# First batch's chain rebuilt in a sketched-attention and FFN kernel: float32 Gram rest, shared key grid, ScalarE rounding the queries, two-step denominator

## The chip, the cores and the metric

The kernel runs on one core of one Trainium2 chip. The time is that of one execution on the device in microseconds (us); a kernel's time is the median of its executions. TensorE is PE below, with PEld its weight loads; VectorE is DVE, ScalarE is ACT, GpSimd is POOL.

## The reference

Attention with a sketched polynomial feature map, then a multiplicative FFN on its output (four batches, four heads, 1088 tokens, head size 32, sketch rank r = 8):

```python
def phi(x):                       # 64 features per token
    a = np.einsum('rd,bhsd->bhsr', S1, x)
    b = np.einsum('rd,bhsd->bhsr', S2, x)
    return np.einsum('bhsi,bhsj->bhsij', a, b).reshape(*x.shape[:-1], r * r)
q_p, k_p = phi(q), phi(k)
kv  = np.einsum('bhsf,bhsd->bhfd', k_p, v)
z   = np.sum(k_p, axis=2)
num = np.einsum('bhsf,bhfd->bhsd', q_p, kv)
den = np.einsum('bhsf,bhf->bhs', q_p, z)[..., None] + 1e-06
x   = (num / den)                 # heads side by side: 4352 x 128
out = ((x @ w1) * (x @ w2)) @ w3 @ w_out
```

S1, S2 and the FFN weights arrive as 64-bit floats.

## The kernel before

The denominator can be near zero, so the kernel computes it in float32 pairs. It needs z, which it gets from the Gram matrix of k (32 x 32 per head) through two small chains, T = S x Gram and N = P x T; P comes from S alone. The Gram itself is exact because k is split into a leading part on a coarse grid and a rest. This is where the change works. "The Gram" below also includes the `kv` products, which sum in the same PSUM tile `ps_kvz`.

```python
def lead(kf, tiles, name, eng):                        # split of k
    x = {n: tiles.tile(kf.shape, t, ...) for n, t in (("k1", BF16), ("k2", F32), ("ks", F32))}
    # peak: row maximum; first: k1 = k rounded to the grid; second:
    nc.vector.tensor_sub(x["k2"], kf, x["k1"])
    eng.tensor_add(x["ks"], kf, x["k1"])
...
def gram(chunks, rows, first, last):
    def products(out, lhs, rhs, start):
        for i, c in enumerate(chunks):
            for h in range(H):                         # the heads rotate innermost
                nc.tensor.matmul(out[h*D:(h+1)*D], c[lhs][rows, h], c[rhs][rows, h], ...)
    products(acc["kv"], "v", "kp", first)              # 64 columns, float32
    products(acc["g2"], "k2", "ks", False)             # 32 columns, float32
    products(acc["g1"], "k1", "k1", False)             # 32 columns, bf16
...
def lead_q():                                          # split of a q tile, on VectorE
    round_to(s["q1"], s["qT"], grid(s["qT"], 128, 8, "q"))
    (nc.vector if lean else nc.gpsimd).tensor_sub(s["q2"], s["qT"], s["q1"])
```

A 64-bit weight becomes float32 in three steps: `words` (two ScalarE activations), `join` (VectorE) and `add` (VectorE). With `signs` a third ScalarE step casts the sign, and the join is one operation; without it VectorE does a shift-and-mask as well.

An FFN step computes `a_ps` and `b_ps` (each one float32 matmul of 512 columns, run as two instructions); ScalarE copies a, VectorE multiplies by b. The third product `ps_o` follows with a lag of 16 steps, since the weights w3 x w_out (`w3o`) have to be built first. The first part of the program has a fixed order; later parts merge several streams of steps in proportion:

```python
run_all([sketch_pairs, ..., kv0, q_tr, kv1, kvr, ..., f[0], n_ay1, ..., n_phT, f[5], n_nd])
run(merge([(1.7, x) for x in f[6:]] + ffn_steps(1, 16), k_steps(1), w_out))
```

## Time and profile before

320.8 us, the median of the runs (319.51 to 322.37). The trace is of a run of 322.2 us, with a span of 320.4 us. The four stages below are read from starts of named matmuls, on the time axis of the views; only PE's end is an end. "Step 7" ends, here and below, with the start of its last instruction, 0.6 us before that is done. The prediction shows the lines themselves.

| stage of the kernel before | from, us | to, us | length |
|---|---|---|---|
| serial chain to the first FFN product | 0 | 41.0 | 41.0 |
| first eight FFN steps (0 to 7) | 41.0 | 62.3 | 21.3 |
| building w3 x w_out ("conversion stage") | 62.3 | 117.3 | 55.0 |
| FFN, with k and q of the later batches between | 117.3 | 315.1 | 197.8 |

In the last stage TensorE is nearly always busy, so every instruction added to it there costs its own time. Until 41.0 us it is busy for 31.0 us, of which some 12 are padding; in the second stage for 18.9 of 21.9 us.

### The profile page before, as it was taken

The page shows a single profiled execution, that of the slowest core. Times are in us where ns is not written, and L with a number is a line of the kernel's source. Part 1 is how long each engine was busy: PE and PEld are TensorE (multiplying, and loading weights), DVE is VectorE, ACT ScalarE, POOL GpSimd, SP SyncE. Part 2 cuts the span into 40 slices and gives each one's busy share as a digit, 9 for nine tenths or more (in the row PEclk, how much of TensorE's full clock was granted, in tenths as well). Part 3 has the DMA queues.
Part 4 walks back from the last instruction along what each step waited for, and adds up shares of the span by engine and source line. Part 5 has one row for each costly group of instructions (what it writes and reads, how often), then busy time and mean ns, then how long its engine had stood idle before and what let it go on. Part 6 is the DMA issues. An engine that isn't in the chain of part 4 may idle for free.

```text
span 320.4 us, 4951 instructions
## 1 busy us (share of the span) xinstructions
PE 293.6 (92%) x1924; PEld 174.4 (54%) x1924; DVE 195.3 (61%) x495; ACT 132.7 (41%) x258; POOL 16.6 (5%) x21
## 2 busy tenths in 40 slices
PE   7866997669998999999999999999999999999992
PEld 5746553257766765465645446555454644444581
DVE  6987867996879638376846626654572572462130
ACT  4313273897998330533332253322324224323231
POOL 2200000100003000010301001000100100000000
PEclk9855699978999999999999999999999999999998
DMA  5998240375743000000000000000000000000000
GB/s 165 337 264 243 94 133 0 105 266 163 246 156 118 0 0 2 33 1 2 3 33 2 0 33 0 2 2 35 2 0 0 33 0 2 33 0 1 35 33 17
DMA packets 15064, 20.77 MB, mean 65 GB/s; under 512 B 4032, under 2 KB 11456, under 8 KB 15040
## 3 DMA queue, kind: packets, MB, share of 16 engines
q1 hardware_dynamic: 15040, 20.46, 19.9%
q8 instruction: 15, 0.25, 0.3%
q14 instruction: 9, 0.07, 0.1%
HBM read 18.22 MB, written 2.23 MB: 64 GB/s over the span
## 4 chain that ended last, share of the span: by engine, by line
PE 73%; ACT 11%; DVE 10%; issue 4%; POOL 1%; DVEq 0%; POOLq 0%
PE ps_o L740 19%; PE a_ps L727 15%; PE b_ps L731 14%; PE ps_w3o L375 3%; PE ps_x L682 3%; ACT cv_c L230 3%; PE ps_kvz L474 3%; PE ps_c L610 3%; PE ps_ph L665 2%; PE ps_c L608 2%; PE idle_ps L184 2%; ACT sgn L236 2%; PE ps_ab L424 2%; ACT cv_m L231 1%; ACT ffa L729 1%
## 5 line engine op out<-in xcount | busy, mean ns | idle before, releaser
L733 DVE TENSOR_TENSOR ab<-ffa,b_ps 128x512 f32<-128x512 f32 (+1 forms) x72 | 47.2, 655 | 62.5 <-PE b_ps L731 56.9
L729 ACT COPY ffa<-a_ps 128x512 f32<-128x512 f32 (+1 forms) x72 | 40.7, 565 | 78.3 <-PE a_ps L727 73.4
L727 PE MATMUL a_ps<-xT,w 128*128 128x512 f32 (+1 forms) x144 | 72.4, 585 | 0.7 <-ACT xT L685 0.7
L731 PE MATMUL b_ps<-xT,w 128*128 128x512 f32 (+1 forms) x144 | 70.5, 571 | 1.3 <-ACT ffa L729 1.3
L740 PE MATMUL ps_o<-ab,w3o 128*128 128x512 f32 (+1 forms) x144 | 70.3, 582 | 0.7 <-ACT ob L743 0.7
L731 PEld LDWEIGHTS b_ps<-xT,w 128*128 128x128 f32 x144 | 26.7, 190 | 29.4 <-issue 22.7
L740 PEld LDWEIGHTS ps_o<-ab,w3o 128*128 128x128 f32 x144 | 24.8, 190 | 22.6 <-issue 20.2
L727 PEld LDWEIGHTS a_ps<-xT,w 128*128 128x128 f32 x144 | 24.4, 192 | 18.0 <-issue 11.7
L375 PE MATMUL ps_w3o<-wo,w3T 128*128 128x128 f32 x128 | 18.0, 293 | 2.4 <-ACT w3T L370 1.7
L264 DVE TENSOR_REDUCE g_q<-qT 128x1 f32<-128x512 f32 (+1 forms) x9 | 5.9, 655 | 23.3 <-ACT qT L578 23.3
L375 PEld LDWEIGHTS ps_w3o<-wo,w3T 128*128 128x128 f32 x128 | 16.9, 205 | 5.5 <-ACT w3T L370 2.8
L667 ACT COPY pT<-ps_ph 128x512 f32<-128x512 f32 (+1 forms) x18 | 9.2, 565 | 15.8 <-PE ps_ph L665 15.8
L231 ACT ACTIVATE cv_m<-raw 128x512 int32<-128x512 uint32 x22 | 15.4, 698 | 0.8 <-DVE w3c L248 0.8
L230 ACT ACTIVATE cv_c<-raw 128x512 f32<-128x512 f32 x22 | 15.4, 706 | 0.0
L610 PE MATMUL ps_c<-Rl,qT 128*128 128x96 f32 (+1 forms) x72 | 15.0, 302 | 0.0
L608 PE MATMUL ps_c<-Rf,q 128*128 128x64 f32 (+1 forms) x72 | 13.2, 276 | 1.4 <-POOL q L584 1.4
L584 POOL TENSOR_TENSOR q<-qT,q 128x512 f32<-128x512 f32 (+1 forms) x6 | 6.4, 1073 | 150.1 <-DVE q L275 150.1
L608 PEld LDWEIGHTS ps_c<-Rf,q 128*128 128x128 f32 (+1 forms) x72 | 11.4, 201 | 4.3 <-issue 2.4
L236 ACT CAST sgn<-cv_c 128x512 f16<-128x512 f32 x17 | 13.4, 790 | 0.1
L184 PE MATMUL idle_ps<-zeros 128*128 128x256 bf16 x52 | 11.9, 420 | 1.6 <-DVE zeros L179 1.6
L665 PEld LDWEIGHTS ps_ph<-ident,ph 128*128 128x128 f32 x68 | 7.9, 143 | 7.6 <-issue 5.9
L432 DVE TENSOR_TENSOR kp<-ps_ab,b_sb 128x1024 f32<-128x1024 f32 x8 | 9.8, 1222 | 3.5 <-ACT b_sb L428 3.5
(169 smaller groups left out, 372.8 us busy)
## 6 DMA issues: line engine op xcount, KB each, us to landing
raw<-in_moe_w_dram SPq DMA_DIRECT2D x20, 512.0 KB, 4.5
k_sb<-in_k_dram SPq DMA_DIRECT2D x4, 512.0 KB, 5.1
v_sb<-in_v_dram SPq DMA_DIRECT2D x4, 512.0 KB, 5.8
q_sb<-in_q_dram SPq DMA_DIRECT2D x4, 512.0 KB, 6.3
out_dram<-oT SPq DMA_DIRECT2D x8, 256.0 KB, 2.0
raw<-in_moe_w_out_dram SPq DMA_DIRECT2D x2, 512.0 KB, 10.4
kr<-in_k_dram SPq DMA_DIRECT2D x4, 32.0 KB, 3.7
vr<-in_v_dram SPq DMA_DIRECT2D x4, 32.0 KB, 6.0
```

Of the source, the lines that this page charges most:

```text
L184: nc.tensor.matmul(idle_ps[:, :n], zeros[:, :128], zeros[:, :n], start=True, stop=True)
L230: nc.scalar.mul(x["c"], hi.bitcast(F32), 2.0 ** -112)
L231: nc.scalar.mul(x["m"].bitcast(I32), lo.bitcast(U32), 2.0 ** -29)
L236: nc.scalar.copy(bview(x["s"].bitcast(F16)[:, 1:], [[2, CW]]), x["c"])
L375: nc.tensor.matmul(ps, w3T[ko][:, c], wo[:, c], start=(c == 0), stop=(c == NC - 1))
L608: nc.tensor.matmul(C[rows, :2, j], s["q2"][:, cols], cols_of(Rf, b), start=True, stop=False, skip_group_check=True)
L610: nc.tensor.matmul(C[rows, :, j], s["qT"][:, cols], cols_of(Rl, b), start=False, stop=True, skip_group_check=True)
L727: nc.tensor.matmul(a_ps[:, :n], w1[:, cols], xT[key], start=True, stop=True)
L729: nc.scalar.copy(a_sb[:, :n], a_ps[:, :n])
L731: nc.tensor.matmul(b_ps[:, :n], w2[:, cols], xT[key], start=True, stop=True)
L733: nc.vector.tensor_mul(ab[:, :n], a_sb[:, :n], b_ps[:, :n])
L740: nc.tensor.matmul(o_ps[g][:, :n], w3o[:, c], ab_sb.pop((g, c))[:, :n], start=c == 0, stop=c == NC - 1)
```

## The change

The intent was to shorten the first batch's chain, and to take work off ScalarE in the conversion stage:

- The Gram's rest is summed in float32 directly: k1 x (k1, k2) as one product of 64 columns, and k2 x k as one of 32. No `ks`, no bf16 part, no symmetrizing afterwards.
- One grid for a batch's k and for the 64-token rest that it carries, loaded into one tile.
- A shorter split of S's words. The prefetch of later inputs waits for VectorE.
- q's rounding moves to ScalarE (two activations with a per-partition bias).
- The denominator's steps are cut in two. FFN steps 6 and 7 come before the conversion of w_out and w3.
- The sign casts of 13 weight chunks give way to shift-and-mask on VectorE.

```diff
-            nc.vector.tensor_sub(x["k2"], kf, x["k1"])
-            eng.tensor_add(x["ks"], kf, x["k1"])
+            for x, (k1, k2) in parts:                   # k and its rest, one grid
+                nc.vector.tensor_sub(k2, x, k1)
...
-            products(acc["kv"], "v", "kp", first)
-            products(acc["g2"], "k2", "ks", False)
-            products(acc["g1"], "k1", "k1", False)
+        def grams(kk, kf, rows, start):
+            for h in range(H):
+                products(acc["g"], h, kk[rows, 0, h], kk[rows, :, h], start=start)
+                if kf is not None:
+                    products(acc["g2"], h, kk[rows, 1, h], kf[rows, h])
+                else:
+                    for x in range(2):
+                        products(acc["g2"], h, kk[rows, 1, h], kk[rows, x, h])
...
+        st.append((0.9, lambda: g_sum(0)))              # a block of its own
+        st.append((0.4, lambda: kv_sum(0, feats[0][1])))
...
-            round_to(s["q1"], s["qT"], grid(s["qT"], 128, 8, "q"))
-            (nc.vector if lean else nc.gpsimd).tensor_sub(s["q2"], s["qT"], s["q1"])
+            nc.scalar.activation(s["q2"], s["qT"], ACT.Identity, bias=g)
+            nc.scalar.activation(s["q1"], s["q2"], ACT.Identity, bias=g, scale=-1.0)
...
-            words, join, add = convert(n, dst, n % 4 != 1)
+            words, join, add = convert(n, dst, signs=False)
...
+             ay1, q_rem, v0, n_nat, v1, ay2, n_tr, pause(22), split, ..., j1, a1, phT, nd, v2, v3,
+             n_grid, n_lead, n_rem, f[0], n_ay1, ..., f[5], n_phT, f[6], n_nd, f[7]])
-    run(merge([(1.7, x) for x in f[6:]] + ffn_steps(1, 16), k_steps(1), w_out))
+    run(merge(ffn_steps(1, 16), k_steps(1), w_out[2:]))
```

The loads, the split of S and the pauses (short runs of padding matmuls) are left out here. v0 to v3 are the ScalarE steps of four weight chunks.

## The prediction

> **What bounds the kernel now.** I read the strip of 40 slices first (one slice is 8.0 us), then the stage table, the timeline of the first 41 us, and the chain of waits from 57 to 118 us.
>
> ```profile
> PE   7866997669998999999999999999999999999992
> DVE  6987867996879638376846626654572572462130
> ACT  4313273897998330533332253322324224323231
> PEclk9855699978999999999999999999999999999998
> ...
> 0.00:41.00 41.00, 31.03 (x323) 24.17 (x323) 31.73 (x110) 12.98 (x27) 3.58 (x12) 0.71 0.69 215
> 41.00:62.90 21.90, 18.91 (x64) 8.47 (x64) 17.55 (x40) 13.10 (x24) 0.92 (x1) 1.00 0.25 75
> 62.90:117.60 54.70, 48.69 (x446) 36.69 (x447) 43.16 (x87) 42.58 (x83) 2.51 (x1) 0.94 0.44 144
> 117.60:315.00 197.40, 194.87 (x1094) 105.10 (x1093) 102.85 (x259) 63.65 (x125) 9.61 (x7) 1.00 0.03 12
> 315.00:320.40 5.40, 0.12 (x2) 0.00 (x0) 0.00 (x0) 0.37 (x1) 0.00 (x0) 0.72 0.11 26
> ```
>
> The table's columns are the stretch, its length, the busy time of PE, PEld, DVE, ACT and POOL, the granted clock, the DMA share, GB/s. From 117.6 us on TensorE is busy for 194.9 of 197.4 us: that stage costs what its matmuls cost. The slack is in front of it. Until 41.0 us, when the first FFN matmul starts, a serial chain (sketch, features of k, Gram, T, N, q) runs, and 12 us of its PE time are padding matmuls. From 62.9 us (second product of FFN step 7 done) to 117.6 us (last `w3o` matmul done) the kernel turns 64-bit words into float32 weights, with DVE and ACT loaded alike; of ACT's work there, 13 casts that take the sign (10.4 us, 799 ns each) are the part that the change drops.
>
> Inside the first stage two things are visibly lost:
>
> ```profile
> 16.44 2.01 issue
> ...
> 18.45 0.21 PE L474 MATMUL ps_kvz<-k 128*32 128x32 bf16 x3 [2.01 <-issue]
> ...
> 13.70:37.60 23.90, 17.42 (x191) 14.39 (x178) 19.22 (x70) 5.70 (x11) 0.00 (x0) 0.50 0.76 241
> ```
>
> In the middle of the Gram sum PE stands 2.01 us with no semaphore to wait for. The record of the instruction queue (q8) has a 16 KB fetch that starts at 16.2 us and takes 1.0 us, while the DMA share is 1.08: I read this as instructions arriving late behind the prefetch of later inputs. And from 13.7 to 37.6 us the clock is 0.50.
>
> **What the Trainium skill says.** "TensorE: Matmul & The Clock Gate", Part 1 (the HAM clock gate): the PE clock is half until a window of about 3.4 us was busy, and falls back after idle ones. The trace agrees: the 0.50 stretch is 23.9 us, seven such windows, and the eight f32 pairs of `ps_c` that take 0.43 us each at 0.50 take 0.22 us at 43 us, where it is 1.00. The padding matmul of 256 columns was spaced 0.22 us apart, the cold rate (256/1.2 GHz); warm, by the same page, it is about 0.11 us (estimate), so the change's 53 pauses cost some 6 us of PE time if warm, 12 if cold, nearly all inside DVE's time.
> "ScalarE: Activation LUTs", "What ACT_TABLE_LOAD costs": a pointer operand costs about 280 ns plus 0.833 ns an element, overlapping 93 ns. So each of the two rounding activations is 0.71 us at 512 elements (estimate); no instruction of that kind is in the trace, but the strided 512-element activation measures 0.706.
> "VectorE: DVE Perf Modes", mode 2x_2P: f32 with one source in SBUF runs at two elements a cycle, two tensors never. The trace agrees: 128x512 shift-and-mask 0.42 us, the two-tensor form 0.68.
> "Trainium Architecture — The Big Picture", what this means for kernel authors: DVE and GpSimd share a port by an exclusive lock. The trace agrees: the 1024-element subtraction took 3.16 us beside GpSimd's 2.51 us `ks` add, 1.22 alone.
>
> **The change part by part, on the path.** I walked the new order of instructions through each engine with these durations (DVE and ACT run in order).
>
> *To the end of the Gram.* S: seven DVE steps become three plus two ScalarE steps, 0.3 us less, but the row maximum now waits for the 32 KB rest of k too (landing 3.7 us after issue, about 6.4 us) and covers 1152 columns: no gain. Then `k1`, `k2`, `kp`, `kp` in turn, without `ks` (1.22) and without the rest's own maximum and grid (0.28 + 2 x 0.19) and before any work on q: DVE's part ends near 14.2 us instead of 16.2. On PE the Gram of a half is 32 f32 products of 64 columns (0.47 us, as kp and v took), 32 of 32 columns (0.28), plus `kv` 0.47: 1.22 us against 0.47 + 0.28 + 0.23 = 0.98. Prefetch is held until DVE passes 14.2 us, so the fetch stall should go (-2.0). With a warm clock the last Gram product ends near 15.7 us (before: 19.2); cold, near 17.8.
>
> *Gram to FFN.* Before: 19.2 to 41.0 us, 21.8. Gone from DVE's serial part: `ym` and its transpose and add (0.5), the maximum of P before T (1.1, now earlier), the two weight conversions in between (0.6 + 0.4 before N's inputs are taken). T, N (0.7 us each less) and the eight `ps_c` pairs (3.4 to 1.8) halve if the clock holds. Added: q's grid (1.05, formerly hidden under the Gram) and two activations (1.4) on the path. Walk, warm: gB 17.7, T pair 20.3, q grid 21.4, N's leading part and q1 22.8, `ps_c` 25.5, denominator 29.1, phi 30.4, then 3.3 us as before: FFN at 33.6. With half clock until the longer pauses warm it: 38. I weigh them to **35.0, 6.0 us earlier**.
>
> *FFN start to the end of step 7.* Before 21.9 us. ScalarE now does two conversions with signs (2 x 1.8) and q's two activations (1.4) between x and the first FFN eviction, so PE waits some 3.4 us after the first step, behind `n_ay1`; afterwards DVE sets the pace (8 evictions of 0.68, two conversions of 1.36, 6.7 of the second q tile), ending 24.1 us after the start: **+2.2**.
>
> *Conversion stage.* ScalarE loses 13 casts: about 46 us become 36. VectorE gains 13 shift-and-mask steps (13 x 0.42 = +5.5), loses `ks` (1.2), the rest's lead (0.9) and two evictions (1.4, done earlier), so of its 39.5 us of this stage's own work about 41.5 remain; the other 6.5 us that it did here were pulled forward from k of batch 2, inflated by the port lock. PE's own work is 42 us (w3 products 14.2, transposes 7.5, 16 FFN products 13.8, k 6.5). Two engines at 42 us of work with three shared PSUM buffers: I expect 47 us. Before: 54.7, less two `ps_o` products done in it (1.7). **-6.0**.
>
> *Rest.* Gram of three batches in the PE-bound stage: 3 x (2 x 0.24 + 0.06) = **+1.6**. The q tiles' path grows by 0.9 us (0.55 on DVE becomes 1.42 on ScalarE); PE waited 0.7 us at 120, 172 and 231 us in exactly this step: **+1.0**, if reordering hides most.
>
> Sum: -6.0 + 2.2 - 6.0 + 1.6 + 1.0 = -7.2; 320.8 - 7.2 = 313.6, say 313.5 us.
>
> **Rivals.**
> *The clock stays half.* The Gram now is all small f32 products, and in the window from 10.4 to 13.8 us just such products (PE 76% busy) preceded the drop. If the pauses do not hold it, FFN starts at 38 to 40: about 317. For it: 64-column products stay cold at 100% busy (30.0 to 34.3 us). Against: 2.35 us of padding inside the window before 37.7 did warm it, and there are now 53 pauses.
> *VectorE takes over the conversion stage from ScalarE.* The strip shows DVE at 6 to 9 tenths there already. If the stage stays at 53 us: about 319. Against: ACT was at 37.5 of 40.6 us from 62.9 to 103.5, and the lock's 1.9 us is gone.
> *Everything holds*: warm clock, conversions at PE's pace (44 us), q's longer path hidden: about 308.5. PE's work after the FFN start and its tail allow no less than some 307.5.
> *The held-back prefetch* (about 4 MB at some 350 GB/s, 15 to 26 us) delays weights: the first new chunk is needed near 33 us, so I give it no time.
>
> **Range and chances.** The clock rival is worth 4 us, the conversion stage 5 up or 3 down, the q path 1: together 308 to 318.5 for eight times in ten. Faster by over 2% means below 314.4, just above my middle: 0.60. Slower than 327 would need several losses at once: 0.02.
>
> **What would show it.** Right: no 2 us gap in the Gram and its end near 16 us; clock 1.00 through most of 14 to 34 us; first `a_ps` at 34 to 36; PE waiting for `q1` about 3 us after FFN step 0; last `w3o` product near 105 to 107; ACT below 80% and DVE above 85% in the conversion stage; PE 0.5 us longer per later batch. Wrong: a clock of 0.5 at `ps_c`, a fetch gap elsewhere, an FFN start after 39 us, or gaps of over 1.5 us before `ps_c` of later q tiles.

## The result, and the profile after

329.06 us (328.45 to 329.98, four runs), correct: **slower by 2.6%**. The ratio is 1.0258, with a 95% interval of 1.0203 to 1.0312. Ratios here are the mean time of one kernel's runs over that of the other's of the same rounds, so not quite the ratio of the medians that are quoted. Executions over 1.5% slower than the fastest of the same kernel are left out of the means.

The strip of 40 slices of the changed kernel (one slice is 8.2 us):

```profile
PE   7768859949999999999999999999999999999992
DVE  7747756499999837268536625735473482362130
ACT  3347444567896442543315354222514524423131
PEclk9996878996999999999999999999999999999998
```

PE is nearly full from the seventh slice on with one dent (the ninth, a 4), DVE is at 9 from the ninth slice to the thirteenth, and ACT is below 9 in every slice but one. The intended shift of load from ScalarE to VectorE is plain to see. The stretches of the prediction's table, in the same columns:

```profile
0.00:20.00 20.00, 14.34 (x293) 11.58 (x294) 11.84 (x43) 5.85 (x14) 0.70 (x6) 1.00 0.81 243
20.00:41.00 21.00, 18.00 (x103) 13.15 (x103) 16.19 (x57) 13.85 (x35) 0.00 (x0) 0.84 0.71 215
41.00:62.90 21.90, 18.11 (x57) 9.39 (x56) 13.29 (x29) 10.11 (x18) 0.00 (x0) 0.84 0.31 96
62.90:117.60 54.70, 49.83 (x481) 36.62 (x480) 48.31 (x106) 38.51 (x73) 0.00 (x0) 0.94 0.39 126
117.60:315.00 197.40, 195.72 (x1172) 105.23 (x1171) 96.68 (x244) 71.26 (x134) 6.44 (x6) 1.00 0.03 10
```

In the fourth row DVE has risen from 43.16 to 48.31 us and ACT has fallen from 42.58 to 38.51, yet PE is as busy as before, 49.83 against 48.69. In the last row PE has 1172 matmuls in place of 1094 in the same time. The totals that PE waited, by tile (us in total, times, longest):

```profile
PE ps_kvz L508 <- DVE kk L492: 4.0, 1, 4.0
PE ps_a L662 <- ACT q L642: 3.6, 2, 2.8
PE ps_kvz L508 <- issue: 2.8, 1, 2.8
```

The third line is the stop inside the Gram: it is still there, and longer (2.01 us before). The second is ScalarE's rounding of q. The first is new: one wait of 4.0 us at 69 us, at the head of the conversion stage. In the kernel before, PE's waits in that stage ended on ScalarE instead. Its two longest, and then the new one:

```profile
64.02 0.66 PE L415 MATMUL ps_kt<-ident,nat 128*128 128x128 f32 x4 [1.14 <-ACT nat L106]
66.73 1.10 PE L424 MATMUL ps_ab<-S12blk,kT 128*128 128x64 f32 x8 [2.06 <-ACT kT L417]
```

```profile
73.14 0.46 PE L508 MATMUL ps_kvz<-kk 128*32 128x64 f32 x8 [4.04 <-DVE kk L492]
```

By stages, from the starts of the same matmuls:

| stage | before | after | change | predicted |
|---|---|---|---|---|
| to the first FFN product | 41.0 | 39.0 | -2.0 | -6.0 |
| FFN steps 0 to 7 | 21.3 | 25.6 | +4.3 | +2.2 |
| end of step 7 to last w3o product | 55.0 | 55.0 | 0.0 | -6.0 |
| last w3o product to PE's end | 197.8 | 201.6 | +3.8 | +2.6 |
| sum | 315.1 | 321.2 | +6.1 | -7.2 |

The traced spans differ by 6.4 us (326.8 against 320.4), the medians by 8.3. The remaining 1.9 us come from the choice of runs: the traced one of before (322.2) lies 1.4 us above its median, that of the changed kernel (328.53) 0.5 us below. The stage times of single traces also scatter: in the variants of the changed kernel below (e4_old_gram apart), FFN starts between 37.6 and 39.4 us. The stop in the Gram, between 1.9 and 3.6 us long there, is one reason and not the only one (e9_ffn_back has a stop of 2.06 us and the latest FFN start). The granted clock is another: it is 0.50 in stretches that lie elsewhere from trace to trace. So a first-stage difference under 2 us between two traces isn't read as an effect.

Where the last stage loses is visible in the chain of waits of batch 2 (start us, length us, what). First the kernel before, then the changed one:

```profile
152.62 0.97 PE ps_kvz L474 x73
153.59 1.05 PE a_ps L727 x2
...
155.51 0.32 PE ps_kvz L474 x19
155.83 1.05 PE ps_o L740 x2
```

```profile
154.26 0.93 PE ps_kvz L508 x46
155.18 1.05 PE ps_o L807 x2
156.24 0.58 PE ps_kvz L508 x32
156.82 1.05 PE a_ps L794 x2
...
158.74 0.89 PE ps_kvz L508 x22
159.62 1.05 PE ps_o L807 x2
```

Half a batch's Gram took 0.97 us in one block. It now takes 0.93 + 0.58 = 1.51 us in two. The rest took 0.32 us and now takes 0.89. And each block breaks the stream of wide matmuls: the pair after a block takes 1.05 us, where an undisturbed pair takes 0.86.

### The profile page after: what moved, and what is told of

Same layout as the page of the kernel before. It is cut to its first block, busy times and chain, and to the rows that moved or that the text cites. A ratio compares the mean times of both kernels' runs of the same rounds, so it can differ in the third digit from the quotient of the medians.

```text
span 326.8 us, 5358 instructions
## 1 busy us (share of the span) xinstructions
PE 301.7 (92%) x2125; PEld 180.4 (55%) x2125; DVE 188.0 (58%) x482; ACT 141.6 (43%) x277; POOL 7.1 (2%) x12
## 4 chain that ended last, share of the span: by engine, by line
PE 82%; DVE 9%; ACT 4%; issue 2%; POOL 1%; POOLq 0%; DVEq 0%
PE ps_o L807 19%; PE a_ps L794 17%; PE b_ps L798 15%; PE ps_kvz L508 5%; PE ps_w3o L403 4%; PE ps_c L672 3%; PE ps_c L670 3%; PE ps_wt L396 3%; PE ps_x L749 3%; PE ps_ab L452 2%; PE ps_ph L732 2%; PE idle_ps L190 2%; DVE ab L800 1%; PE ps_ot L817 1%; ACT q L642 1%
## 5 line engine op out<-in xcount | busy, mean ns | idle before, releaser
L794 PE MATMUL a_ps<-xT,w 128*128 128x512 f32 (+1 forms) x144 | 73.5, 592 | 0.7 <-ACT xT L752 0.7
L798 PEld LDWEIGHTS b_ps<-xT,w 128*128 128x128 f32 x144 | 27.4, 193 | 29.7 <-issue 25.7
L807 PEld LDWEIGHTS ps_o<-ab,w3o 128*128 128x128 f32 x144 | 24.9, 190 | 21.0 <-issue 19.8
L276 DVE TENSOR_REDUCE g_q<-qT 128x1 f32<-128x512 f32 (+1 forms) x9 | 5.9, 655 | 27.5 <-ACT qT L630 27.5
L403 PEld LDWEIGHTS ps_w3o<-wo,w3T 128*128 128x128 f32 x128 | 15.7, 192 | 3.4 <-issue 2.6
L670 PE MATMUL ps_c<-Rf,q 128*128 128x64 f32 (+1 forms) x72 | 14.3, 293 | 2.6 <-POOL q L646 1.5
L672 PE MATMUL ps_c<-Rl,qT 128*128 128x96 f32 (+1 forms) x72 | 16.1, 319 | 0.0
L403 PE MATMUL ps_w3o<-wo,w3T 128*128 128x128 f32 x128 | 16.0, 275 | 0.0
L670 PEld LDWEIGHTS ps_c<-Rf,q 128*128 128x128 f32 (+1 forms) x72 | 12.3, 215 | 5.5 <-POOL q L646 2.4
L190 PE MATMUL idle_ps<-zeros 128*128 128x256 bf16 x77 | 13.3, 340 | 1.7 <-DVE zeros L185 1.7
L508 PE MATMUL ps_kvz<-kk 128*32 128x64 f32 x256 | 8.6, 236 | 4.0 <-DVE kk L492 4.0
L672 PEld LDWEIGHTS ps_c<-Rl,qT 128*128 128x128 f32 (+1 forms) x72 | 12.1, 217 | 0.0
```

What stands on the lines that cost most here:

```text
L190: nc.tensor.matmul(idle_ps[:, :n], zeros[:, :128], zeros[:, :n], start=True, stop=True)
L403: nc.tensor.matmul(ps, w3T[ko][:, c], wo[:, c], start=(c == 0), stop=(c == NC - 1))
L508: nc.tensor.matmul(out[h * D:(h + 1) * D], lhs, rhs, start=start, stop=stop, skip_group_check=True)
L670: nc.tensor.matmul(C[rows, :2, j], s["q2"][:, cols], cols_of(Rf, b), start=True, stop=False, skip_group_check=True)
L672: nc.tensor.matmul(C[rows, :, j], s["qT"][:, cols], cols_of(Rl, b), start=False, stop=True, skip_group_check=True)
L794: nc.tensor.matmul(a_ps[:, :n], w1[:, cols], xT[key], start=True, stop=True)
```

## The experiments

Fifteen kernels ran, all correct. The median of the kernel before was 321.14, 320.86, 321.21 and 321.26 us in the four groups. "F" below is the start of the first FFN product, "W" the last w3o product, and F to W is the two middle stages together (76.3 us before, 80.5 after). The last stage is W to PE's end.

| run | built on | median us | ratio to before, 95% interval |
|---|---|---|---|
| changed kernel | | 329.06 | 1.0258 (1.0203 to 1.0312) |
| e1_order | changed | 325.99 | 1.0154 (1.0134 to 1.0174) |
| e2_join | changed | 324.44 | 1.0119 (1.0082 to 1.0156) |
| e3_order_join | changed | 324.2 | 1.0098 (1.0076 to 1.0121) |
| e4_old_gram | changed | 331.23 | 1.0313 (1.0274 to 1.0353) |
| e5_signs | e3 | 324.47 | 1.0119 (1.0096 to 1.0142) |
| e6_q_dve | e3 | 320.45 | 0.9965 (0.9926 to 1.0004) |
| e7_v23 | e3 | 322.46 | 1.0039 (0.9994 to 1.0084) |
| e8_hold | e3 | 325.82 | 1.0164 (1.0125 to 1.0204) |
| e9_ffn_back | e6 | 319.0 | 0.9924 (0.9892 to 0.9956) |
| e10_all | e9 | **317.35** | **0.9873** (0.984 to 0.9907) |
| e11_before_few | before | 327.41 | 1.018 (1.0146 to 1.0213) |
| e12_hold2 | e6 | 320.66 | 0.9977 (0.995 to 1.0003) |
| e13_all_signs | e10 | 317.9 | 0.9914 (0.9867 to 0.9962) |
| e14_before_fwd | before | 323.09 | 1.0061 (1.0031 to 1.0092) |
| e15_after_back | changed | 325.25 | 1.0114 (1.0069 to 1.016) |

### The Gram: order and blocks

My theory was that three things make the Gram dear in the PE-bound stage: three products of one head in a row in the rest, a block more per half, and the additional columns. Rival: the rebuilt Gram costs what its columns cost, whatever the order.

**e1_order** issues the products by kind, with the heads rotating:

```diff
-            for h in range(H):
-                products(g, h, kk0, kk); products(g2, h, kk1, k)
+            for each kind of product:
+                for h in range(H): products(...)
```

> Only the order of the Gram products changes: first all products of one kind over the four heads (so that successive matmuls go to different 32-column groups), then the next kind. Theory A (the Gram costs what it costs because products of one head follow each other in one column group): the block of 64 products of a half falls from 0.93 to about 0.75 us, the rest's 32 from 0.89 to about 0.40; per batch 2 x 0.18 + 0.5 = 0.85 us, over the three batches where TensorE is the bound and the first one in the chain some 3 us: about 326 against 329. Rival B (the extra TensorE time after 118 us is the q tiles' longer path, not the Gram): blocks unchanged or no gain, 329.

Measured 325.99 us. The rest falls from 0.89 to 0.48 us; the half only from 0.93 to 0.88. The last stage falls from 201.6 to 200.6 us. In the trace the 24 products of the rest start within 0.65 us when each head's six instructions stand together, and within 0.25 us when the heads rotate (batches 1 to 3 in the trace of e3_order_join, which has the same order).

**e2_join** puts the `kv` products back into the Gram's block for batches 1 to 3:

```diff
-        st.append((0.9, lambda: g_sum(0)))
-        st.append((0.4, lambda: kv_sum(0, ...)))
+        st.append((1.3, lambda: both(0)))
```

> Only for batches 1 to 3: the k features' products (kv) run in one block with the Gram's, as in the kernel before, instead of in a block of their own. Theory A2 (each extra block of small products between 512-column products costs a break of some 0.2 us plus 0.1 us in the kv block itself): 2 halves x 0.3 us x 3 batches = 1.8 us: about 327.2. Rival: blocks cost nothing by themselves: 329.

Measured 324.44 us, a larger gain than expected. A half is now one block of 1.38 us. The last stage fell from 201.6 to 199.7 us. In the traces another 1.4 us came in the first stage and 1.6 between F and the end of step 7, which the edit doesn't touch. That is scatter: the stop is 0.8 us shorter, and the half-clock stretches lie elsewhere.

**e3_order_join** has both edits.

> Both edits at once. If both theories hold and add: 329 - 3 - 1.8 = about 324.3, and the time from the last w3o product to the end falls by some 3 us from 207. If the q path is to blame: 329.

Measured 324.2 us, as expected, though the two single gains (3.1 and 4.6 us) don't add up to this one (4.9). In the last stage they do: 1.0 and 1.9 us alone, 2.8 together. Its chain of batch 2:

```profile
153.30 1.33 PE ps_kvz L508 x92
154.63 1.05 PE a_ps L795 x2
...
156.55 0.48 PE ps_kvz L508 x32
157.03 1.05 PE ps_o L808 x2
```

A half is 1.33 us and the rest 0.48; the last stage is 198.8 us. So order and blocks make up most of what the last stage lost. The remainder, 1.33 against 0.97, is by elimination the extra columns; e4_old_gram, below, is without them and its last stage is another 1.0 us shorter.

**e4_old_gram** goes back to the bf16 leading part and `ks` inside the changed kernel, with the joined blocks and one raw buffer fewer (5 instead of 6, for room):

```diff
-                products(acc["g"], h, kk0, kk); products(acc["g2"], h, kk1, k)
+                products(acc["g2"], h, k2, ks);  products(acc["g1"], h, k1, k1)   # by kind
+            nc.scalar.mul(ym, acc["g2"], 0.5)    # and its transpose and add in the finish
```

> The Gram of the kernel before put back into the changed one (bf16 leading part, remainder times (k + leading part), made symmetric by a transpose), products by kind, kv in the same block for batches 1 to 3, one raw buffer less for room. If the new Gram is the whole cost of the TensorE-bound stage: 2.0 us per batch less there, 6 us in all plus about 1 in the first chain, less 1.2 us for the sum it needs again: about 323. If the Gram is not what costs there: 329 or more.

A miss: 331.23 us. The last stage did come to 197.76 us, close to the 197.81 of before, so its loss is nearly all the Gram. But the first chain became 6 us longer (F at 44.9 us): VectorE stood 9.05 us before 24.9 us for `ym`, which my edit had put on ScalarE behind the change's 16 small activations that fill R. The edit made that wait; the time says nothing about the change.

### ScalarE, the casts and q

**e5_signs** brings the 13 casts back to ScalarE (on e3).

```diff
-            words, join, add = convert(n, dst, signs=False)
+            words, join, add = convert(n, dst, n % 4 != 1)
```

> On top of e3 (Gram products by kind, kv in the same block): the casts that take the sign on ScalarE put back for three of four weight chunks, as in the kernel before. Theory A (in the changed kernel VectorE is late at the head of the conversion stage: 10.1 us from FFN step 7 to the first w3 transpose, 5.7 before; from then on TensorE is the bound): one shift-and-mask step of 0.42 less per cast chunk brings the first transpose some 1 us earlier, 324.2 becomes about 323. Rival (ScalarE bounded that stage and does so again with 13 casts of 0.8 us): the stage from step 7 to the last w3o product stays at 55 or grows, 325 to 328.

324.47 us, no difference that the intervals show. The traces say why: from the end of step 7 to the last w3o product PE is idle for 5.05 us in e3 and 5.06 us here. With the casts on ScalarE it waits 0.6 us longer for ScalarE's kT and 0.4 for its w3T, and 0.65 less for VectorE's kk. The part of the change that was meant to unload ScalarE gains nothing here: it moves the wait.

**e6_q_dve** rounds q on VectorE again (on e3):

```diff
-            nc.scalar.activation(s["q2"], s["qT"], ACT.Identity, bias=g)
-            nc.scalar.activation(s["q1"], s["q2"], ACT.Identity, bias=g, scale=-1.0)
+            round_to(s["q1"], s["qT"], g)
```

> On top of e3: q's leading part rounded on VectorE in one instruction as in the kernel before, signs of the factors put back. Theory A (the two activations stand in ScalarE's queue behind two weight conversions, so TensorE waits 2.8 us for q1 of the second tile, and the first chain is 0.9 us longer): FFN start 0.9 us earlier, step 7 some 3 to 4 us earlier relative to today, about 321. Rival (VectorE is the bound between FFN start and the w3 stage, so 0.55 us more per tile on it costs as much): 324.

320.45 us, as expected: 3.8 us less than e3, almost all of it between F and the end of step 7 (24.9 to 20.8 us). With the wait, a stretch of 6.8 us at half clock in these steps is gone too.

**e7_v23** leaves q on ScalarE and moves the conversions v2 and v3 from in front of the rounding to behind the first FFN step (on e3):

```diff
-             ..., phT, nd, v2, v3, n_grid, n_lead, n_rem, f[0], n_ay1, n_ay2, j2, a2,
+             ..., phT, nd, n_grid, n_lead, n_rem, f[0], v2, n_ay1, n_ay2, v3, j2, a2,
```

> On top of e3: the ScalarE part of the third and fourth weight chunk moved from before q's rounding of the second tile to after it and after FFN step 0. Theory A (the wait for q1 comes from the queue order on ScalarE, 3.6 us of conversions in front): the wait of 2.8 us before the second tile's first product goes, step 7 ends 2 to 3 us earlier relative to the FFN start, about 321.7. Rival (VectorE or the third and fourth chunk itself are then late): 324.

322.46 us, 0.8 us short of what was expected. F to the end of step 7 is 20.3 us. So the wait was the queue on ScalarE in front of the two activations more than the activations themselves.

### The stop in the Gram

The prediction read the stop as instructions arriving late behind the prefetch. **e8_hold** meant to hold all prefetch until the Gram's finishing step:

```diff
+            if b == 1: nc.vector.memset(<one element of the k, v and q tile>, 0.0)
-             ..., kvr, q_tr, load_more, pause(5), sketch_R, sketch_Pa, fin1, T_mm,
+             ..., kvr, q_tr, pause(5), sketch_R, sketch_Pa, fin1, load_more, T_mm,
```

> On top of e3: every later input, also k and v of the second batch (whose loads the changed kernel let go at 7 us), waits until VectorE has done the Gram's last step, so the DMA engines are quiet while the Gram runs. Theory A (TensorE runs out of fetched instructions at its 228th weight load in every kernel so far, and the fetch of the next 16 KB is held up by data traffic): the gap of 2.1 to 3.8 us falls below 1.2 us, FFN start 1.5 to 2.5 us earlier, about 322. Rival (the fetch takes that long whatever the traffic): gap stays above 2 us, and later weights cost time: 324 or more.

A failed edit. With `load_more` behind the finishing step, the loads of batch 2 inside that step took the free buffers and were issued at 7.1 and 10.5 us. The DMA share stayed at 0.97 to 1.13 from 12 to 16 us. 325.82 us says nothing about congestion.

**e12_hold2** does it properly (on e6, with the same one-element memsets):

```diff
         # in the Gram's finishing step
+            if b == 0: load_more()
             if b + 2 < B: load_in("k", b + 2); load_in("v", b + 2)
```

> The changed kernel with Gram reordered and joined and q on VectorE, with every load of later inputs truly held until VectorE has finished the Gram's finishing step. What I predicted blind: no prefetch, no stop. Theory of congestion: DMA share from 13 to 18 us falls below 0.3 and the stop (2.7 us in the same kernel without the hold) falls to 1 us or less; FFN start 1.5 us earlier, about 319 us. Rival, the fetch has its own latency: stop still 2 to 3 us, FFN start the same or later for the late loads, 320.5 to 322 us.

The stretches from 15 to 18 us, first of e6_q_dve, then of e12_hold2 (same columns as above, the DMA share second to last):

```profile
15.00:16.00 1.00, 0.32 (x24) 0.21 (x13) 0.00 (x0) 0.00 (x0) 0.00 (x0) 1.00 1.11 300
16.00:17.00 1.00, 0.00 (x0) 0.00 (x0) 0.00 (x0) 0.00 (x0) 0.00 (x0) 1.00 1.00 290
17.00:18.00 1.00, 0.22 (x17) 0.22 (x20) 0.00 (x0) 0.00 (x0) 0.00 (x0) 1.00 0.95 229
```

```profile
15.00:16.00 1.00, 0.00 (x0) 0.00 (x0) 0.00 (x0) 0.00 (x0) 0.00 (x0) 1.00 0.28 107
16.00:17.00 1.00, 0.00 (x0) 0.00 (x0) 0.00 (x0) 0.00 (x0) 0.00 (x0) 1.00 0.00 0
17.00:18.00 1.00, 0.29 (x21) 0.29 (x24) 0.00 (x0) 0.00 (x0) 0.00 (x0) 1.00 0.00 0
```

With the DMA engines idle the stop is as long as ever: 2.88 us, against 2.46 in e6_q_dve. The prediction's cause for it is refuted. In all seventeen traces a 16 KB instruction fetch starts between 0.8 us before and 1.1 us after PE comes to a stand, takes 0.9 to 1.2 us, and PE goes on 2.4 to 2.7 us after the fetch began. With idle DMA engines (e12_hold2) that last figure is 2.2 us, so traffic is at most a few tenths of it. That PE waits for this fetch is likely, and no run shows it by an edit.

**e11_before_few** asks what sets the place of the stop. In all kernels PE stood after 227 or 228 recorded weight loads. Here the kernel before has 12 paddings of 512 columns in place of 24 of 256 columns, and two sets of small matmuls go behind the Gram:

```diff
-    idle(24)
+    idle(12, 512)
-    ..., ab1, q_nat, sketch_P_mm, r_peak, ..., kv0, q_tr, kv1, kvr, idle(8), ...
+    ..., ab1, q_nat, r_peak, ..., kv0, kv1, kvr, sketch_P_mm, q_tr, idle(8), ...
```

> The kernel before, with fewer PE instructions ahead of the Gram's end (24 paddings of 256 columns become 12 of 512; sketch_P's and q's transposes go behind the Gram), so that weight load 228, at which all kernels stood still, comes after the Gram. Theory of a limit in instructions: the 2.0 to 2.2 us stop leaves the Gram, the Gram ends about 2 us earlier, FFN starts 1 to 2 us earlier: 319 to 320 us, and a stop, if any, appears at the same count after the Gram. Rival (the stop comes at a time near 16 us, not at a count): the stop stays near 16.4 us inside the Gram and nothing is gained, 320.8 us.

```profile
17.08 0.22 PE L474 MATMUL ps_kvz<-k 64*32 64x32 bf16 x2
20.37 0.21 PE L474 MATMUL ps_kvz<-k 64*32 64x32 bf16 x2 [3.07 <-issue]
```

This is the timeline of PE (start, length, engine, what, and in brackets the wait in front). The stop comes after 228 recorded weight loads (227 in the kernel before), but begins 0.9 us later, and now stands in front of the Gram's last two matmul instructions instead of its last 23. So it goes with a count of instructions, not with a time or with what is being computed. Nothing was gained: the two instructions still had to wait, and the moved steps came late (F at 47.5 us, 327.41 us in all). The expected time was wrong.

### The order of FFN steps and conversions

After e7 the largest loss was in front of the first transpose of w3: from the end of step 7 it took 10.1 us in the changed kernel and 5.7 in the kernel before. VectorE in the changed kernel there (timeline):

```profile
62.36 0.69 DVE L800 TENSOR_TENSOR ab<-ffa,b_ps 128x512 f32<-128x512 f32 x1 [2.16 <-PE b_ps L798]
65.28 0.69 DVE L800 TENSOR_TENSOR ab<-ffa,b_ps 128x512 f32<-128x512 f32 x1 [2.24 <-PE b_ps L798]
65.89 0.42 DVE L256 TENSOR_SCALAR wo<-cv_c 128x512 int32<-128x512 int32 x1
...
71.87 1.22 DVE L492 TENSOR_TENSOR kk<-k_sb,kk 128x1024 f32<-128x1024 f32 x1
```

VectorE waits 4.4 us for PE in the FFN steps 6 and 7, with the conversions behind them in its queue. Then it works without a break, and PE waits 4.0 us for the last line shown. The engines take turns.

**e9_ffn_back** puts steps 6 and 7 back into the merged stream (on e6):

```diff
-             ..., n_dens2, f[4], n_phi, w_out[1][1], f[5], n_phT, f[6], n_nd, f[7]])
+             ..., n_dens2, f[4], n_phi, w_out[1][1], f[5], n_phT, n_nd])
-    run(merge(ffn_steps(1, 16), k_steps(1), w_out[2:]))
+    run(merge([(1.7, x) for x in f[6:]] + ffn_steps(1, 16), k_steps(1), w_out[2:]))
```

> The changed kernel with its Gram reordered and joined, q rounded on VectorE as in the 320.45 us run, and FFN steps 6 and 7 put back behind the start of the weight conversions, where the kernel before had them. Theory: the 10.1 us between the end of step 7 and the first w3 transpose (5.7 in the kernel before) is PE idle because those steps are done before VectorE has a chunk ready; with 13.8/16 x 2 = 1.7 us of FFN products a step as filler, that stretch falls by 2 to 3.4 us: 317 to 318.5 us, ratio to before about 0.99. Rival: VectorE's work sets the end of the conversion stage, so the filler only trades places: the last w3o product stays near 115 us and the time at 320 to 320.5.

319.0 us, 0.5 over the range expected; F to W falls from 76.3 to 74.2 us.

**e10_all** adds the edit of e7.

> The same with the conversions v2 and v3 put behind q's rounding and the first FFN step as well. Undone alone, that gave F to f7 20.3 us instead of 24.9 and 322.46 against 324.2 us. With q on VectorE most of that wait is gone already, so theory: 0 to 0.7 us less than the run before it, 317 us; rival: 1.5 us less again, 315.5, if the two gains add.

**317.35 us**, 1.65 us less than e9: the rival's "the gains add" came nearer (the two intervals just overlap). This version beats both kernels: 1.3% under the kernel before, with the interval below 1, though inside the 2% band. Its stretches up to the FFN, to the last w3o product, and to PE's end (each bound 0.2 us late):

```profile
0.00:38.60 38.60, 32.23 (x392) 25.70 (x393) 28.64 (x101) 16.23 (x43) 0.70 (x6) 0.82 0.80 243
38.60:111.70 73.10, 67.33 (x554) 44.92 (x554) 62.53 (x136) 49.26 (x93) 0.00 (x0) 0.98 0.41 123
111.70:311.00 199.30, 197.16 (x1182) 106.66 (x1180) 101.22 (x255) 63.44 (x123) 6.45 (x6) 1.00 0.03 12
```

F to W is 73.1 us (76.3 before), and the wait for `kk` in this kernel is

```profile
61.82 0.65 PE L508 MATMUL ps_kvz<-kk 128*32 128x64 f32 x32 [0.89 <-DVE kk L492]
```

0.89 in place of 4.0 us.

**e13_all_signs** asks whether the casts matter in this better order (e10 with the edit of e5).

> The fastest version (317.35 us) with the 13 casts that take the sign put back on ScalarE in place of the shift-and-mask steps on VectorE. Theory: the prediction's -6.0 us for the conversion stage was wrong in its bound; ScalarE did not set that stage, so the exchange is worth under 1 us in either order: 317 to 318.3 us. Rival: it was only masked by the order of the FFN steps, and ScalarE, some 10 us fuller, sets the stage again: 320 us or more, F to the last w3o product 2.5 us longer than 73.1.

317.9 us, no difference from e10_all that the intervals show. F to W is 72.75 us, but this trace has no half-clock stretch there and that of e10_all has one of 3.4 us (63.0 to 66.4), so the two lengths can't be compared to better than some 1.5 us (an estimate: half of the 3.04 us for which PE is busy in it). The rival's 320 us and its 2.5 us more from F to W are not seen; a gain of some 1 us from the exchange of casts for shift-and-mask isn't excluded.

**e14_before_fwd** moves FFN steps 6 and 7 forward in the kernel before:

```diff
-             ..., f[5], n_nd])
+             ..., f[5], f[6], n_nd, f[7]])
-    run(merge([(1.7, x) for x in f[6:]] + ffn_steps(1, 16), k_steps(1), w_out))
+    run(merge(ffn_steps(1, 16), k_steps(1), w_out))
```

> The kernel before with FFN steps 6 and 7 moved ahead of the conversions of w_out and w3, as the change has them. Theory: the order alone loses 1 to 3 us, 322 to 324 us, with 8 to 10 us between the end of step 7 and the first w3 transpose in place of 5.7. Rival: VectorE's and ScalarE's amount of work sets the stage, 320.8 us.

323.09 us: +1.8 against the 321.26 of its group, as the theory said. End of step 7 to the first w3 transpose is 10.95 us, and from step 7 to W PE is idle for 8.9 us in place of 6.0.

**e15_after_back** makes the opposite edit, that of e9, in the changed kernel alone.

> The changed kernel with only those two FFN steps put back behind the start of the conversions. Theory: 1 to 3 us of its 329.06 us return: 326 to 328 us. Rival: 329 us.

325.25 us, 3.8 us less than the changed kernel's 329.06 (in another group), more than expected. F to W falls from 80.5 to 76.9 us.

The order acts in part through the clock. At the head of the conversion stage it is 0.50 for 10.2 us in e14_before_fwd (64.9 to 75.1) and for 6.8 in the kernel before (68.2 to 75.0); for 3.4 us in e15_after_back (65.9 to 69.3) and for 6.8 in the changed kernel (71.9 to 78.7). PE is busy for 6.9, 6.1, 3.1 and 5.4 us of these stretches, and the half clock can cost half of that (estimate): up to 0.4 us of the 1.8 in the first pair and 1.1 of the 3.8 in the second.

## Why the prediction was wrong

The prediction said 313.5 us (308 to 318.5); it was 329.06. The step that failed most is the conversion stage. Its sum, step by step:

**"To the end of the Gram", "the fetch stall should go (-2.0)": wrong in its cause.** VectorE's part ended at 14.1 us, as said (14.2). But the stop stayed and grew to 2.75 us, and the Gram ended at 20.0, not near 15.7. That is 2.75 of the 4.3 us; the Gram's own length and its start make the rest. e12_hold2 shows that the stop stays without the prefetch, and e11_before_few that it goes with a count of instructions. I had the fetch in view and took a busy DMA beside it for its cause. (It starts at 16.0 us on the axis of the views, 0.4 us before PE stands, not at 16.2.)

**"Gram to FFN": nearly right.** 19.1 us against the 17.9 of the warm walk. The clock was 1.00 until 27.5 us and 0.50 from there to 34.35, just over the eight `ps_c` pairs, which took 3.5 us instead of 1.8: the rival "the clock stays half", in one part. The windows in front of such a drop were not idle, as the prediction had it: PE was busy for 2.17 of the 3.41 us before 27.5 us, and for 2.49 of 3.41 before the drop at 13.6 us in the kernel before. With the stop that makes -2.0 us for F in place of -6.0.

**"FFN start to the end of step 7", +2.2: mechanism right, size off.** The wait for `q1` was foreseen, at about 3 us, and was 2.82 us long. The estimate of 0.71 us for an activation held: 0.71 and 0.72 measured. The rest of the +4.3 lies in a clock of 0.50 from 44.6 to 51.4 us, in which PE was busy for 6.75 us (some 3.4 us lost, by estimate); two waits of the kernel before, 2.9 us together, had shrunk to 0.3. The wait of 2.8 us comes just in front of that stretch; that it is its cause is argued, not shown. e6_q_dve and e7_v23 both take the stage back to 20 to 21 us.

**"Conversion stage", -6.0: this step failed most, in its bound and in what PE waited for.** I added up PE's own work as 42 us, beside a row that gave PE as busy for 48.69 of 54.70 us. The predicted 47 us equal 48.69 less the two `ps_o` products (1.7): PE without any idle time at all, although the text called it two engines sharing at 42. The terms I had taken too small, with what they occupied in the trace of before (from each start to the next start, or to the instruction's own end): w3o products 16.45 us (14.2), transposes 8.6 (7.5), FFN products 15.0 (13.8). Most of that gap is the clock, which the row gives as 0.94 and the sum took as full: it was 0.50 from 68.2 to 75.0 us, PE was busy for 6.05 us of this, and some 3 us of its busy time are therefore the half clock (estimate). In the changed kernel, where they all ran at 1.00, the w3o products occupy 14.3 us.

ScalarE was what PE waited for: 5.6 of its 6.0 us of idle time in the trace of before ended on ScalarE. But these 6.0 us were all that relief could give, and the change moved the wait to VectorE instead of ending it: PE is idle for 4.9 us after, 4.0 of them for VectorE's `kk`. e5_signs and e13_all_signs put the 13 casts back and lost nothing that the intervals show. What the change did do besides was to make work for PE (`ps_kvz` from 2.5 to 5.1 us, and one more `ps_o` pair) and to reorder the FFN steps, which made the wait for `kk` so long. I had listed the reorder only as two evictions fewer for VectorE. Alone it costs 1.8 us in the kernel before (e14_before_fwd), and 3.8 us come back in the changed kernel when it is undone (e15_after_back), part of it by way of the clock.

**"Gram in the PE-bound stage", +1.6: mechanism right, size off by a factor of nearly four.** I counted 0.24 us for a half and 0.06 for the rest. Measured per batch: 2 x (1.51 - 0.97) = 1.08 for the halves, 0.89 - 0.32 = 0.57 for the rest, and 2 x 0.19 = 0.38 for one more break per half, 2.0 us in all. For the two batches of the last stage this is 4.1 us (batch 1 lies in the conversion stage). The stage grew by 3.8 us with one `ps_o` pair (0.86 us) fewer in it, so by 4.7 like for like. I had priced instructions by their mean in the old order, where heads rotate, and not read the new loop's order or the cut into two blocks.

**"The q tiles' path", +1.0: nearly no sign of it.** In the last stage PE waited twice for q, 0.76 us each at 177.1 and 236.5 us; before, 0.69 us each at 172.4 and 231.4. Both are waits for GpSimd's subtraction, the step after the rounding, and the wait at 120 us that the prediction names isn't in the trace.

Of the rivals, "VectorE takes over the conversion stage" came nearest: the stage stayed at 55 us. PE's own work fills 49.8 us of it, and the longest wait of the rest is for VectorE, late at the head by order.

With the errors of order undone (e10_all), F to W is 73.1 us against the predicted 72.5 (76.3 - 6.0 + 2.2), and the last stage 199.3 against 200.4. The 3.4 us by which F is late (38.4 against 35.0) are then most of what separates e10_all's 317.35 from the predicted 313.5. That F to W comes so close is luck: the casts, on which the -6.0 rested, are not what shortened it. PE is busy for 67.6 us between F and W in the kernel before and in e10_all alike; its idle time fell from 9.0 to 5.8 us, while the clock was 0.50 for 6.8 us before and for 3.4 us in e10_all. What removed those waits stays partly open. The changed kernel no longer has `ks`, the rest's own split and the subtraction beside GpSimd on VectorE, some 4 us by the prediction's terms; no run takes these away one by one. Open as well is how to move the stop to a place where PE waits anyway.

## What to carry to other kernels

Before a stage is promised a gain, subtract the bottleneck engine's busy time from the stage's length: at an unchanged clock no relief of another engine can give more than that remainder, and then look for the engine that the wait will move to. Where the row shows a clock under 1.00, as here, part of the busy time itself is the clock. Price new instructions in their new order, with the blocks they are cut into, since the same count cost 0.89 or 0.48 us here. And when steps move ahead of others in an engine's fixed order, ask what that engine could have done in its waits; two FFN steps moved forward cost more than 13 removed casts gained.

## What the Trainium skill lacked or had wrong

- What it costs when an engine's instructions run out: "Runtime: NRT & Kernel Launch", Instruction fetch mechanics, says that instructions are refilled in blocks of 16 KiB and that the cost of crossing a boundary is mostly hidden. "Perfetto Trace Analysis" counts the fetch as a part of its Stage 1 (Instruction Decode), without a figure. Here PE stood after 227 or 228 recorded weight loads in every kernel, for 1.7 to 3.6 us, with a 16 KB fetch of 0.9 to 1.2 us beginning near the stop's start, and for 2.9 us with the DMA share at 0.00 from 16 us on (e12_hold2).
- "TensorE: Matmul & The Clock Gate", Part 3 (The mechanism): it says that weight loads overlap with matmuls in flight only when the row group differs. In the Gram's rest all heads read the same 64 rows and differ in their columns; 24 products start within 0.25 us when the column group changes from one to the next, and within 0.65 us when it stays for six. (The table at the end of the same page does promise a gain for distinct column groups.) The same page's Part 1 says that starts are never less than about 25 ns apart, without the exception that its Part 3 makes for tiles in different row groups; with changing column groups the trace has most of them 6 to 8 ns apart.
- The break where narrow products interrupt wide ones: "TensorEngine Tiling (Array Packing)", Key Properties, says that changing the tiling mode drains the TensorE, without a figure. The pair of 512-column instructions after a Gram block takes 1.05 us here, an undisturbed pair 0.86; that this is that drain, no run shows.
